# The relu of an ELU layer written to SBUF instead of its PSUM bank, in an attention + MLP kernel ordered by a planner

## The chip, the cores and the metric

One core of one Trainium2 chip runs the whole program. The metric is the device time of one execution in microseconds; a kernel is represented by the median of its runs. A profile of one execution shows every instruction of the five engines: PE (matmul), DVE (VectorE), ACT (ScalarE), POOL (GpSimd) and SP (DMA issue).

## The reference

The kernel computes block-sparse causal attention (4 batches, 8 heads, 768 tokens, head dimension 64; each query keeps 6 of 24 chunks of 32 keys) and feeds the result to a two-layer MLP with an ELU between the layers:

```
ub   = sum_d max(q*k_min, q*k_max)          # one bound per chunk
sel  = top 6 chunks by ub (causal)
attn = softmax(mask(q @ k.T / 8)) @ v
x    = attn, heads side by side              # 3072 x 512
h    = x @ w_in                              # 512 -> 2048
g    = where(h > 0, h, exp(min(h, 0)) - 1)   # ELU
out  = g @ w_out                             # 2048 -> 512
```

## The kernel before

The work is cut into units. A unit is a pair of heads of one batch; there are 16 of them, and each has two halves of 384 query rows. A unit's half goes through loading and transposing K and Q, the chunk bounds on PE (line 580), the top-6 selection on DVE (lines 597 to 620), copies on POOL that put the selection beside the bf16 operands (lines 548, 631), scores on PE (L672), exp on ACT (L699), the causal triangle on POOL (L718), the product with V on PE (L731), the division on DVE (L744, L747, tile `on`), and a transpose of the result (PE L756, ACT L759, tile `xT`). Counted over units and halves there are 32 operations `on`.

Four units make a batch. Its MLP runs in two halves of 384 rows. For each of 16 blocks of 128 hidden columns (`fc`) four matmuls make `h` in a PSUM bank (L781, tile `psH`; batch 3 takes two blocks at a time in a two-bank tile `psS`), ACT writes `e = exp(h)` to SBUF (L791), and the ELU is finished as `min(e - 1, relu(h))`. The result goes to `gT` in SBUF, from which the down projection (L838, tiles `psM`, `psMT`) reads 4 blocks per step, and ACT copies the sums out (L846). There are 96 such blocks in batches 0 to 2. Before the change they come in two forms, chosen by the table `BOTH`:

- in `BOTH` (48 blocks): ACT applies relu to the PSUM bank in place (L796), then one DVE operation reads `e` from SBUF and the bank (L799);
- otherwise (48 blocks): two DVE operations, each reading the bank (L820: `t = max(e - 1, h)`, L825: `gT = min(max(h, 0), t)`).

In both forms the bank is released by the last DVE operation (`free=bh + [e]`, `free=bh + [t]`). There are 3 banks of kind `H`, 3 buffers of `e`, 3 of `t` and 3 of `gT`. Batch 3 (`FAST`) uses a third form (L809, L814).

The order of all work is made by a planner (class `Plan`). Each step is added with an engine, an estimated duration, a rank `prio`, what it reads and writes, and which buffers it takes and frees. `order()` repeatedly starts the step that can start first, and among those that wait for one engine the one of lowest rank. Steps marked `port=True` and all POOL steps exclude each other in the plan; DVE steps without the mark run beside POOL. Instructions are then emitted in this order, and each engine's queue, the DMA queues of SP and POOL too, executes in order.

Of the kernel before, what the change touches and what calls it, by code (L numbers as in the profile page):

```python
# [10 lines left out]
AOT = mybir.AluOpType  # L11
AF = mybir.ActivationFunctionType
# [5 lines left out]
S = 768  # L18
# [10 lines left out]
HALF = S // 2  # L29
# [6 lines left out]
SPLIT = (0, 1, 2, 3)  # L36
GATES = {(2, 0): (0, 1, 2, 3), (2, 1): (4, 5, 6, 7)}

BOTH = {0: (0, 1, 4, 5, 8, 9, 12, 13), 1: (0, 1, 2, 3, 4, 5, 8, 9, 10, 11, 12, 13), 2: (1, 5, 9, 13), 3: ()}


def WHEN(q_in, left, out):
# [9 lines left out]
LATER = {4: 0}  # L52
RATES = (232.0, 232.0, -1.4, 0.75)
MERGE = (False, False, False, True)

DUMP = None

# [6 lines left out]
class Plan:  # L64
# [17 lines left out]
    def add(self, eng, dur, prio, emit, reads=(), writes=(), alloc=(), free=(), lat=None, tag="",  # L82
# [33 lines left out]
        self.ops.append(o)  # L116
        return o

    def order(self):
# [12 lines left out]
        waiting = {}  # L132
        for o in ops:
            waiting.setdefault(o.eng, [])
            engines[o.eng] = self.BEGIN
            if not o.left:
                waiting[o.eng].append(o)
        n_left = len(ops)
        port = {"POOL": 0.0, "DVE": 0.0}
        out = []  # L140
        while n_left:
            best = None
            for e, t in engines.items():
                cand = None
                for o in waiting[e]:
                    r = max(t, o.ready)
                    if o.port and o.eng in port:
                        r = max(r, port["DVE" if o.eng == "POOL" else "POOL"])
                    ok = True
                    for h in o.alloc:  # L150
                        fs = free_slots[h[0]]
                        if not fs:
                            ok = False
                            break
                        r = max(r, min(fs)[0])
                    if not ok:
                        continue
                    key = (r, o.prio, o.n) if r > t else (t, o.prio, o.n)
                    if cand is None or key < cand[0]:
                        cand = (key, o, r)  # L160
                if cand is not None and (best is None or cand[2] < best[2]):
                    best = cand
            assert best is not None, "no operation can start"
            _, o, r = best
            slots = []
            for h in o.alloc:
                fs = free_slots[h[0]]
# [24 lines left out]
            n_left -= 1  # L192
        return out
# [3 lines left out]
def kernel(  # L197
# [9 lines left out]
    nc = tc.nc  # L207
# [178 lines left out]
    def pair_prep(u):  # L386
# [52 lines left out]
        add("POOL", 0.13 + 0.00096 * S, pr + 1.0,  # L439
            lambda: nc.gpsimd.tensor_copy(out=tiles[vx][:, :, 0:D], in_=tiles[vd]),  # L440
            reads=[vd, "ones"], writes=[(vx, i) for i in range(2)], alloc=[vx], free=[vd])

    def first_prep(u, hf):
# [60 lines left out]
            return x.rearrange("q (j p) -> q p j", j=4)  # L504
        add("PE", TURN, pr, turn(bk, at_k), reads=[(hk, i0), "ident"], writes=[bk[0]], alloc=bk, free=fk)
        for hd in range(2):
            add("ACT", act(HALF), pr,
                lambda hd=hd: nc.scalar.activation(
                    out=tiles[kb][0:64, hd, a:b].rearrange("q (p j) -> q p j", j=4),
                    in_=tok(ps(bk, None, None)[64 * hd:64 * hd + 64, :]), func=AF.Copy),  # L510
                reads=[bk[0]], writes=[(kb, hf, hd), (bk[0], "turn")], alloc=[] if hf or hd else [kb])
# [26 lines left out]
        add("POOL", 0.13 + 0.00096 * HALF, pr + 1.0,  # L538
            lambda: nc.gpsimd.tensor_copy(
                out=tiles[vx].rearrange("p (h n) d -> p h n d", h=2)[:, :, 3 * hf:3 * hf + 3, 0:D],  # L540
                in_=tiles[sv][:, iv].rearrange("p (h n d) -> p h n d", h=2, d=D)),
# [3 lines left out]
    def cast(pr, w, what, **kw):  # L545
        def f():
            o, i = what()
            nc.gpsimd.tensor_copy(out=o, in_=i)  # L548
        add("POOL", 0.13 + 0.00096 * w, pr, f, **kw)

    def quad_sel(g, hf):

# [210 lines left out]
    def mlp(b, hf):  # L763
        tail = b == B - 1
        if True:
# [3 lines left out]
            for fc in range(0, NFC, step):  # L769
# [3 lines left out]
                def view(bh=bh):  # L773
                    return tiles[bh[0]][:, :, 0:HALF] if tail else ps(bh, [P, 1, HALF], F32)

                def up(view=view, fc=fc, c0=c0):
# [14 lines left out]
                    lambda e=e, view=view: nc.scalar.activation(  # L791
                        out=tiles[e][:, 0:step], in_=view(), func=AF.Exp),
                    reads=[bh[0]], writes=[(e, 0)], alloc=[e])
                if both:
                    add("ACT", act(step * HALF), pr,
                        lambda view=view: nc.scalar.activation(out=view(), in_=view(), func=AF.Relu),  # L796
                        reads=[bh[0]], writes=[bh[0]])
                    add("DVE", dve(step * HALF), pr,
                        lambda e=e, view=view, fc=fc, gt=gt: nc.vector.scalar_tensor_tensor(  # L799
                            out=tiles[gt][:, fc:fc + step, :], in0=tiles[e][:, 0:step], scalar=1.0, in1=view(),  # L800
                            op0=AOT.subtract, op1=AOT.min),
                        reads=[(e, 0), bh[0]], writes=[(gt, fc + i) for i in range(step)],
                        alloc=[gt] if fc == 0 else [], free=bh + [e])
                    continue
                t, = new("t")
                fast = FAST[b]
                if fast:
                    add("DVE", 0.32 + 0.00021 * step * HALF, pr,
                        lambda e=e, t=t: nc.vector.tensor_scalar(  # L809
                            out=tiles[t][:, 0:step], in0=tiles[e][:, 0:step], scalar1=1.0, scalar2=1.0,  # L810
                            op0=AOT.min, op1=AOT.subtract),
                        reads=[(e, 0)], writes=[t], alloc=[t], free=[e], port=True)
                    add("DVE", dve(step * HALF), pr,
                        lambda t=t, view=view, fc=fc, gt=gt: nc.vector.tensor_tensor(  # L814
                            out=tiles[gt][:, fc:fc + step, :], in0=tiles[t][:, 0:step], in1=view(), op=AOT.max),
                        reads=[t, bh[0]], writes=[(gt, fc + i) for i in range(step)],
                        alloc=[gt] if fc == 0 else [], free=bh + [t])
                    continue
                add("DVE", dve(step * HALF), pr,
                    lambda e=e, t=t, view=view: nc.vector.scalar_tensor_tensor(  # L820
                        out=tiles[t][:, 0:step], in0=tiles[e][:, 0:step], scalar=1.0, in1=view(),
                        op0=AOT.subtract, op1=AOT.max),
                    reads=[(e, 0), bh[0]], writes=[t], alloc=[t], free=[e])
                add("DVE", dve(step * HALF), pr,
                    lambda t=t, view=view, fc=fc, gt=gt: nc.vector.scalar_tensor_tensor(  # L825
                        out=tiles[gt][:, fc:fc + step, :], in0=view(), scalar=0.0, in1=tiles[t][:, 0:step],
                        op0=AOT.max, op1=AOT.min),
                    reads=[t, bh[0]], writes=[(gt, fc + i) for i in range(step)],
                    alloc=[gt] if fc == 0 else [], free=bh + [t])
            for tt in range(3):  # L830
                bm = bank("MT" if tail else "M")
                for part in range(4):
                    pr = mpos(b, hf) + 2 + 2 * (4 * tt + part) / 12

                    def down(bm=bm, tt=tt, part=part, gt=gt):
# [2 lines left out]
                            nc.tensor.matmul(pm, lhsT=tiles[gt][:, fc, 128 * tt:128 * tt + 128],  # L838
                                             rhs=w_out_sb[:, fc, :], start=(fc == 0), stop=(fc == NFC - 1))
                    add("PE", 4 * 0.2165, pr, down,  # L840
                        reads=[("w_out", part)] + [(gt, fc) for fc in range(4 * part, 4 * part + 4)],
                        writes=[(bm[0], part)], alloc=bm if part == 0 else [],
                        free=[gt] if tt == 2 and part == 3 else [])
                osb, = new("osb")
# [92 lines left out]
```

## Time and profile before

| | |
|---|---|
| median of 3 runs (lowest, highest) | 280.38 us (280.21, 285.49) |
| span of the profiled execution, first to last instruction | 278.4 us |
| outside the span (median less span) | 2.0 us |
| busy PE / DVE / ACT / POOL | 266.7 / 204.2 / 201.4 / 128.0 us |
| granted PE clock | full in all 40 slices |
| DMA | 29.82 MB, mean 107 GB/s |

The profiled execution has no separate time beside its span; the 2.0 us are taken as what lies around it. Busy times are unions of instruction intervals, so an engine whose instructions overlap by their pipelines can look fuller than it is. Idle time of an engine matters only where the engine that sets the end waits for it.

### The profile page before, as it was taken

The numbers are of one execution on the slowest core, as the hardware profiler recorded it, in microseconds if no ns is written. First come the engines' busy times: TensorE is split into PE (matmuls) and PEld (weight loads), VectorE is DVE, ScalarE is ACT, GpSimd is POOL, SyncE is SP. The second block draws the span as 40 slices with busy tenths as digits, with TensorE's granted clock in tenths as the row PEclk, the third lists the DMA queues.
The fourth block names the chain that finished last, engine by engine and source line by source line (L and its number), as shares of the span: only waits on it lengthen the run. The fifth ranks groups of instructions, "written<-read, shape, count | busy, mean of one in ns | idle before, by whom it ended". The sixth has DMA issues, their size and how long they took to land.

```text
span 278.4 us, 7242 instructions
## 1 busy us (share of the span) xinstructions
PE 266.7 (96%) x2732; PEld 164.0 (59%) x2732; DVE 204.2 (73%) x546; ACT 201.4 (72%) x381; POOL 128.0 (46%) x235
## 2 busy tenths in 40 slices
PE   7989899989999999999999999999999999999994
PEld 7968566644565556655665656565565556555541
DVE  6876965799999989999989588657856434767610
ACT  2879899946699697999899958685868564544311
POOL 5668863356797797966965625102320201000000
PEclk9999999999999999999999999999999999999999
DMA  7999999988998599999497101101101111101122
GB/s 187 232 211 188 197 203 207 146 131 163 189 171 156 73 143 201 165 163 170 87 164 114 38 2 38 40 0 40 39 4 38 40 39 40 38 0 40 38 75 75
DMA packets 111330, 29.82 MB, mean 107 GB/s; under 512 B 101056, under 2 KB 108224, under 8 KB 111296
## 3 DMA queue, kind: packets, MB, share of 16 engines
q1 hardware_dynamic: 106656, 24.78, 48.4%
q0 software_dynamic: 4224, 4.19, 9.2%
q8 instruction: 21, 0.34, 0.6%
q10 hardware_dynamic: 416, 0.39, 0.5%
q14 instruction: 13, 0.11, 0.1%
HBM read 27.26 MB, written 6.29 MB: 121 GB/s over the span
## 4 chain that ended last, share of the span: by engine, by line
PE 68%; ACT 15%; DVE 6%; DMA 4%; issue 3%; SPq 1%; POOL 0%; ACTq 0%; DVEq 0%
PE psM L838 20%; PE psH L781 15%; PE psS L781 7%; PE psMT L838 7%; PE psS L672 7%; ACT pt L699 7%; PE psO L731 5%; ACT e L791 3%; PE psS L580 3%; DMA gT<-in_v_dram 2%; DMA gT<-in_k_dram 2%; ACT psH L796 1%; ACT xT L759 1%; DVE gT L799 1%; PE psT L756 1%
## 5 line engine op out<-in xcount | busy, mean ns | idle before, releaser
L699 ACT ACTIVATE pt<-psS 128x768 bf16<-128x768 f32 (+1 forms) x120 | 91.5, 799 | 4.1 <-PE psS L672 2.6
L781 PE MATMUL psH<-xT,w_in_sb 128*128 128x384 bf16 x384 | 75.2, 325 | 1.6 <-ACT xT L759 0.9
L838 PE MATMUL psM<-w_out_sb,gT 128*128 128x512 bf16 x288 | 72.5, 379 | 0.4 <-DVE gT L825 0.2
L781 PEld LDWEIGHTS <-w_in_sb 128*128 128x128 bf16 x512 | 47.6, 97 | 34.8 <-issue 4.0
L791 ACT ACTIVATE e<-psH 128x384 f32<-128x384 f32 x96 | 48.3, 519 | 22.4 <-PE psH L781 21.9
L838 PEld LDWEIGHTS <-gT 128*128 128x128 bf16 x384 | 36.2, 98 | 35.0 <-DVE gT L825 0.6
L718 POOL TENSOR_SCALAR_AFFINE_SELECT pt<-pt 128x256 bf16<-128x256 bf16 (+1 forms) x56 | 29.0, 519 | 56.7 <-ACT pt L699 55.7
L672 PE MATMUL psS<-rhs,lhs 88*128 88x384 bf16 (+4 forms) x304 | 51.5, 283 | 1.6 <-ACT pt L699 0.9
L672 PEld LDWEIGHTS <-lhs 88*128 88x128 bf16 x304 | 27.8, 97 | 15.8 <-issue 1.5
L631 POOL COPY rhs<-selt 24x192 bf16<-24x192 bf16 (+2 forms) x56 | 25.5, 456 | 21.9 <-DVE selt L620 18.6
L799 DVE SCALAR_TENSOR_TENSOR gT<-e,psH 128x384 bf16<-128x384 f32 x48 | 25.6, 539 | 13.3 <-ACT psH L796 13.2
L731 PEld LDWEIGHTS <-pt 128*128 128x128 bf16 x672 | 27.8, 98 | 11.3 <-issue 3.8
L548 POOL CAST rhs<-qt 64x768 bf16<-64x768 f32 (+1 forms) x40 | 28.5, 711 | 12.3 <-ACT qt L526 6.1
L820 DVE SCALAR_TENSOR_TENSOR t<-e,psH 128x384 bf16<-128x384 f32 x48 | 25.9, 543 | 9.6 <-ACT e L791 9.2
L731 PE MATMUL psO<-vext,pt 128*128 128x65 bf16 x672 | 30.2, 194 | 1.7 <-DVE gT L799 1.1
L791 ACT ACTIVATE e<-psS 128x768 f32<-128x768 f32 x16 | 13.0, 810 | 19.0 <-PE psS L781 19.0
L825 DVE SCALAR_TENSOR_TENSOR gT<-psH,t 128x384 bf16<-128x384 f32 x48 | 25.9, 543 | 0.8
L796 ACT ACTIVATE psH<-psH 128x384 f32<-128x384 f32 x48 | 25.1, 528 | 0.0
L781 PE MATMUL psS<-xT,w_in_sb 128*128 128x384 bf16 x128 | 23.2, 326 | 0.0
L548 POOL CAST lhs<-kt 64x768 bf16<-64x768 f32 x24 | 19.6, 819 | 6.8 <-DVE kt L409 3.7
L838 PE MATMUL psMT<-w_out_sb,gT 128*128 128x512 bf16 x96 | 22.5, 379 | 0.0
L759 ACT ACTIVATE xT<-psT 128x384 bf16<-128x384 bf16 x32 | 16.5, 515 | 4.5 <-PE psT L756 4.4
(66 smaller groups left out, 293.4 us busy)
## 6 DMA issues: line engine op xcount, KB each, us to landing
out_dram<-osb SPq DMA_DIRECT2D x24, 256.0 KB, 2.0
vd<-in_v_dram SPq DMA_DIRECT2D x12, 384.0 KB, 5.2
stage<-in_k_dram SPq DMA_DIRECT2D x48, 96.0 KB, 3.4
stage<-in_q_dram SPq DMA_DIRECT2D x48, 96.0 KB, 3.6
w_in_sb<-in_moe_w_in_dram POOLq DMA_DIRECT2D x4, 512.0 KB, 11.5
w_out_sb<-in_moe_w_out_dram POOLq DMA_DIRECT2D x4, 512.0 KB, 8.8
gT<-in_v_dram SPq DMA_DIRECT2D x16, 96.0 KB, 4.3
gT<-in_k_dram SPq DMA_DIRECT2D x6, 192.0 KB, 5.5
```

What stands on the lines that cost most here:

```text
L548: nc.gpsimd.tensor_copy(out=o, in_=i)
L672: nc.tensor.matmul(p_s[:, hd, pc:pc + w], lhsT=tiles[pt_["kb"]][0:64 + NCH, hd, 128 * kb:128 * kb + 128], rhs=tiles[pt_["qb"]][0:64 + NCH, ...
L699: lambda bs=bs, pt=pt, wtot=wtot, lo=lo, at=at: nc.scalar.activation(out=tiles[pt][:, :, lo:lo + wtot], in_=tiles[bs[0]][:, :, at:at + wto ...
L718: nc.gpsimd.affine_select(out=a, in_=a, compare_op=AOT.is_ge, fill=0.0, base=0, pattern=pat, channel_multiplier=-1)
L731: nc.tensor.matmul(po[:, hd, qi, :], lhsT=tiles[pt][:, hd, off:off + 128], rhs=tiles[pt_["vx"]][:, 6 * hd + kb, :], start=(kb == 0), stop= ...
L781: nc.tensor.matmul(ph, lhsT=w_in_sb[:, kk, f0:f0 + 128], rhs=tiles[XT[4 * b + kk]][:, c0:c0 + HALF], start=(kk == 0), stop=(kk == NKK - 1))
L791: lambda e=e, view=view: nc.scalar.activation(out=tiles[e][:, 0:step], in_=view(), func=AF.Exp),
L796: lambda view=view: nc.scalar.activation(out=view(), in_=view(), func=AF.Relu),
L799: lambda e=e, view=view, fc=fc, gt=gt: nc.vector.scalar_tensor_tensor(out=tiles[gt][:, fc:fc + step, :], in0=tiles[e][:, 0:step], scalar=1 ...
L820: lambda e=e, t=t, view=view: nc.vector.scalar_tensor_tensor(out=tiles[t][:, 0:step], in0=tiles[e][:, 0:step], scalar=1.0, in1=view(), op0 ...
L825: lambda t=t, view=view, fc=fc, gt=gt: nc.vector.scalar_tensor_tensor(out=tiles[gt][:, fc:fc + step, :], in0=view(), scalar=0.0, in1=tiles ...
L838: nc.tensor.matmul(pm, lhsT=tiles[gt][:, fc, 128 * tt:128 * tt + 128], rhs=w_out_sb[:, fc, :], start=(fc == 0), stop=(fc == NFC - 1))
```

## The change

In batches 0 to 2 the relu of a block is now written to a `t` buffer in SBUF (bf16), by ACT for blocks in `BOTH` (line 839 of the changed kernel) and by DVE otherwise (line 843). The PSUM bank is freed by this relu. One DVE operation (line 847) then reads `e` and the relu, both from SBUF. `BOTH` is smaller: 32 blocks instead of 48. The planner gets 88 seeds (`SHIFTS`), each of which moves the rank of one window of steps or of all windows a little before the order is made; two duration estimates change (POOL copies from 0.00096 to 0.00084 us per element, and the ACT copy of K in batch 0 to 0.495 us), and the four parts of a down projection are made to depend on each other in turn. No other arithmetic changes, but the order of instructions does, on all engines and in the SP queue.

```diff
-BOTH = {0: (0, 1, 4, 5, 8, 9, 12, 13), 1: (0, 1, 2, 3, 4, 5, 8, 9, 10, 11, 12, 13), 2: (1, 5, 9, 13), 3: ()}
+BOTH = {0: (0, 4, 8, 12), 1: tuple(range(0, 16, 2)), 2: (1, 5, 9, 13), 3: ()}
+SHIFTS = (711345, 710489, 927914, ...
+    def shift(self, seeds):
+        ops = self.ops
+        n = len(ops)
+        for seed in seeds:
...
+            if draw() < 0.1:            # windows of 5 to 64 steps over the whole list
...
+                    for o in ops[j:j + w]:
+                        o.prio += m
...
+            else:                       # one window, of one engine in half of the draws
...
+                for o in ops[a:a + w]:
+                    if not one or o.eng == ops[a].eng:
+                        o.prio += m
     def order(self):
         ops = self.ops
+        self.shift(SHIFTS)
...
-                if both:
-                    add("ACT", act(step * HALF), pr,
-                        lambda view=view: nc.scalar.activation(out=view(), in_=view(), func=AF.Relu),
-                        reads=[bh[0]], writes=[bh[0]])
+                fast = FAST[b]
+                if both or not fast:
+                    r, = new("t")
+                    if both:
+                        add("ACT", act(step * HALF), pr,
+                            lambda view=view, r=r: nc.scalar.activation(out=tiles[r][:, 0:step], in_=view(), func=AF.Relu),
+                            reads=[bh[0]], writes=[r], alloc=[r], free=bh)
+                    else:
+                        add("DVE", dve(step * HALF), pr,
+                            lambda view=view, r=r: nc.vector.tensor_scalar(
+                                out=tiles[r][:, 0:step], in0=view(), scalar1=0.0, scalar2=None, op0=AOT.max),
+                            reads=[bh[0]], writes=[r], alloc=[r], free=bh)
                     add("DVE", dve(step * HALF), pr,
-                        lambda e=e, view=view, fc=fc, gt=gt: nc.vector.scalar_tensor_tensor(
-                            out=tiles[gt][:, fc:fc + step, :], in0=tiles[e][:, 0:step], scalar=1.0, in1=view(),
-                            op0=AOT.subtract, op1=AOT.min),
+                        lambda e=e, r=r, fc=fc, gt=gt: nc.vector.scalar_tensor_tensor(
+                            out=tiles[gt][:, fc:fc + step, :], in0=tiles[e][:, 0:step], scalar=1.0,
+                            in1=tiles[r][:, 0:step], op0=AOT.subtract, op1=AOT.min),
...
-                        alloc=[gt] if fc == 0 else [], free=bh + [e])
+                        alloc=[gt] if fc == 0 else [], free=[e, r])
...
-                    lambda e=e, t=t, view=view: nc.vector.scalar_tensor_tensor(
-                        out=tiles[t][:, 0:step], in0=tiles[e][:, 0:step], scalar=1.0, in1=view(),
-                        op0=AOT.subtract, op1=AOT.max),
-                    reads=[(e, 0), bh[0]], writes=[t], alloc=[t], free=[e])
...
```

More of the change, by code (lines that the diff above doesn't have):

```diff
@@ L54 @@
 MERGE = (False, False, False, True)
+SHIFTS = (711345, 710489, 927914, 266268, 840942, 852719, 674714, 873198, 676568, 189402, 749298, 506023, 526548,
[6 rows of a table added]
 DUMP = None
@@ L117, in add, with draw @@
         return o
+    def shift(self, seeds):
+        ops = self.ops
+        n = len(ops)
+        for seed in seeds:
+            x = [seed]
+            def draw():
+                x[0] = (6364136223846793005 * x[0] + 1442695040888963407) % 2 ** 64
+                return (x[0] >> 40) / 16777216.0
+            draw(), draw()
+            if draw() < 0.1:
+                amp = draw() * 0.8
+                j = 0
+                while j < n:
+                    w = 5 + int(draw() * 60)
+                    m = amp * (draw() - 0.5) * 2
+                    for o in ops[j:j + w]:
+                        o.prio += m
+                    j += w
+            else:
+                a = int(draw() * n)
+                v = draw()
+                w = 1 + int(v * v * v * 80)
+                amp = draw()
+                amp = 0.1 + 2.4 * amp * amp
+                m = amp * (draw() - 0.5) * 2
+                one = draw() < 0.5
+                for o in ops[a:a + w]:
+                    if not one or o.eng == ops[a].eng:
+                        o.prio += m
     def order(self):
         ops = self.ops
+        self.shift(SHIFTS)
         for o in ops:
@@ L438, in pair_prep @@
         fetch(0.5, 393.0, 205.0, pl + 1.2, vload, [vd], alloc=[vd], reads=late)
-        add("POOL", 0.13 + 0.00096 * S, pr + 1.0,
+        add("POOL", 0.13 + 0.00084 * S, pr + 1.0,
             lambda: nc.gpsimd.tensor_copy(out=tiles[vx][:, :, 0:D], in_=tiles[vd]),
@@ L506, in first_prep @@
         for hd in range(2):
-            add("ACT", act(HALF), pr,
+            add("ACT", 0.495, pr,
                 lambda hd=hd: nc.scalar.activation(
@@ L537, in first_prep @@
                  reads=[qt], writes=[(qb, hf, hd)], alloc=[] if hf or hd else [qb])
-        add("POOL", 0.13 + 0.00096 * HALF, pr + 1.0,
+        add("POOL", 0.13 + 0.00084 * HALF, pr + 1.0,
             lambda: nc.gpsimd.tensor_copy(
@@ L548, in f @@
             nc.gpsimd.tensor_copy(out=o, in_=i)
-        add("POOL", 0.13 + 0.00096 * w, pr, f, **kw)
+        add("POOL", 0.13 + 0.00084 * w, pr, f, **kw)
     def quad_sel(g, hf):
@@ new lines, in mlp @@
+                if both or not fast:
[9 more added lines that the diff above has]
+                            reads=[bh[0]], writes=[r], alloc=[r], free=bh)
+                    add("DVE", dve(step * HALF), pr,
+                        lambda e=e, r=r, fc=fc, gt=gt: nc.vector.scalar_tensor_tensor(
+                            out=tiles[gt][:, fc:fc + step, :], in0=tiles[e][:, 0:step], scalar=1.0,
+                            in1=tiles[r][:, 0:step], op0=AOT.subtract, op1=AOT.min),
+                        reads=[(e, 0), r], writes=[(gt, fc + i) for i in range(step)],
+                        alloc=[gt] if fc == 0 else [], free=[e, r])
@@ L804, in mlp @@
                     continue
                 t, = new("t")
[L806 to L818, printed above, removed]
@@ L819, in mlp @@
-                add("DVE", dve(step * HALF), pr,
-                    lambda e=e, t=t, view=view: nc.vector.scalar_tensor_tensor(
-                        out=tiles[t][:, 0:step], in0=tiles[e][:, 0:step], scalar=1.0, in1=view(),
-                        op0=AOT.subtract, op1=AOT.max),
-                    reads=[(e, 0), bh[0]], writes=[t], alloc=[t], free=[e])
[L824 to L827, printed above, removed]
+                add("DVE", 0.32 + 0.00021 * step * HALF, pr,
+                    lambda e=e, t=t: nc.vector.tensor_scalar(
+                        out=tiles[t][:, 0:step], in0=tiles[e][:, 0:step], scalar1=1.0, scalar2=1.0,
+                        op0=AOT.min, op1=AOT.subtract),
+                    reads=[(e, 0)], writes=[t], alloc=[t], free=[e], port=True)
@@ L828, in mlp @@
+                add("DVE", dve(step * HALF), pr,
+                    lambda t=t, view=view, fc=fc, gt=gt: nc.vector.tensor_tensor(
+                        out=tiles[gt][:, fc:fc + step, :], in0=tiles[t][:, 0:step], in1=view(), op=AOT.max),
                     reads=[t, bh[0]], writes=[(gt, fc + i) for i in range(step)],
@@ L840, in mlp @@
                     add("PE", 4 * 0.2165, pr, down,
-                        reads=[("w_out", part)] + [(gt, fc) for fc in range(4 * part, 4 * part + 4)],
+                        reads=[("w_out", part)] + [(gt, fc) for fc in range(4 * part, 4 * part + 4)]
+                        + ([(bm[0], part - 1)] if part else []),
                         writes=[(bm[0], part)], alloc=bm if part == 0 else [],
```

1 line of the change is left out of this document (removed), and 6 rows, old and new, of the table SHIFTS.

## The prediction

> **What bounds the kernel now.** I began with the page: the span, the busy shares and the 40 slices.
>
> ```profile
> span 278.4 us, 7242 instructions
> PE 266.7 (96%) x2732; PEld 164.0 (59%) x2732; DVE 204.2 (73%) x546; ACT 201.4 (72%) x381; POOL 128.0 (46%) x235
> PE   7989899989999999999999999999999999999994
> DVE  6876965799999989999989588657856434767610
> ACT  2879899946699697999899958685868564544311
> POOL 5668863356797797966965625102320201000000
> ```
>
> PE is full almost everywhere, so a shorter time must come from PE's few gaps, and any wait that makes PE idle is added to the end. DVE's row is the second thing to see: near 9 for the first half, loose after it. I then cut the span at PE's gaps and at two operations `on` (L747), the 8th and the 24th of the 32, which start where these rows begin.
>
> ```profile
> core 0: us, PE busy (x) PEld busy (x) DVE busy (x) ACT busy (x) POOL busy (x), PEclk, DMA share, GB/s
> 0.00:36.00 36.00, 32.40 (x568) 27.02 (x569) 27.34 (x109) 26.48 (x60) 25.63 (x61) 1.00 1.06 203
> 36.00:60.00 24.00, 21.95 (x234) 13.96 (x232) 16.71 (x35) 22.28 (x42) 11.39 (x20) 1.00 1.18 177
> 60.00:146.00 86.00, 83.77 (x931) 49.87 (x930) 81.54 (x228) 71.83 (x137) 66.17 (x113) 1.00 0.93 152
> 146.00:175.00 29.00, 29.00 (x272) 17.28 (x270) 22.80 (x62) 22.88 (x45) 13.81 (x23) 1.00 0.25 47
> 175.00:278.40 103.40, 99.54 (x736) 55.93 (x733) 55.84 (x116) 57.98 (x98) 10.97 (x20) 1.00 0.10 37
> ...
> 59.38 0.55 DVE L747 TENSOR_TENSOR on<-psO,rc 128x384 bf16<-128x384 f32 x1
> ...
> 174.65 0.56 DVE L747 TENSOR_TENSOR on<-psO,rc 128x384 bf16<-128x384 f32 x1
> ```
>
> Before 36 us loading and transposing set the pace. From 36 to 60 us ACT is full (22.28 of 24) and PE loses 2.05. From 60 to 146 us three engines share the load: PE idles 2.23 us, DVE is busy 81.54 of 86 (idle 4.46), POOL 66.17 (77%). From 146 us PE has no gap until its last instruction, so nothing lost before can be won back there. Only 2.05 + 2.23 = 4.3 us of idle PE time between 36 and 146 us, and 3.6 before, are there to be won; the tail after PE's last instruction stays.
>
> **The part that the change names: the bank.** The groups by line say what PE waited for ahead of an up projection, and what one operation of each kind lasts.
>
> ```profile
> L781 PE MATMUL psH<-xT,w_in_sb 128*128 128x384 bf16 x384 | 75.2, 325 | 1.6 <-ACT xT L759 0.9 <-DVE gT L799 0.2 <-DVE gT L825 0.2
> L799 DVE SCALAR_TENSOR_TENSOR gT<-e,psH 128x384 bf16<-128x384 f32 x48 | 25.6, 539 | 13.3 <-ACT psH L796 13.2
> L820 DVE SCALAR_TENSOR_TENSOR t<-e,psH 128x384 bf16<-128x384 f32 x48 | 25.9, 543 | 9.6 <-ACT e L791 9.2
> L825 DVE SCALAR_TENSOR_TENSOR gT<-psH,t 128x384 bf16<-128x384 f32 x48 | 25.9, 543 | 0.8
> L796 ACT ACTIVATE psH<-psH 128x384 f32<-128x384 f32 x48 | 25.1, 528 | 0.0
> ```
>
> PE idled 1.6 us in all before 384 matmuls, and the last DVE operation, which holds the bank, ended 0.4 us of that (L799 and L825). So releasing the bank early is worth 0.4 us directly. More is possible only through the new order, up to the 4.3 us above.
>
> **ACT and DVE.** `BOTH` goes from 48 to 32 blocks, so ACT loses 16 relus (0.53 us each by L796), and DVE gets 16 operations more: 160 instead of 144. In the 36 to 60 us stretch ACT carries 4 relus of batch 0 where it carried 8 (counted in the two orders between the 4th and 8th `xT`); 4 x 0.53 = 2.1 us of ACT. Part of PE's 2.05 us there follows ACT; I take 1.0 us of gain, bounds 0 and 2.
>
> For the middle I counted both instruction orders between the 8th and the 24th `on`. DVE has 34 + 22 + 22 = 78 MLP operations there before, and 32 relus + 55 `gT` = 87 after, and one more K/Q transpose. What they cost back to back, and what PE work moves, is read from starts.
>
> ```profile
> 36.23 0.56 DVE L825 SCALAR_TENSOR_TENSOR gT<-psH,t 128x384 bf16<-128x384 f32 x1
> 36.70 0.45 DVE L614 TENSOR_TENSOR selv<-ubt,thr 128x288 bf16<-128x288 f32 x1
> 37.07 0.55 DVE L820 SCALAR_TENSOR_TENSOR t<-e,psH 128x384 bf16<-128x384 f32 x1
> ...
> 140.06 0.33 PE psS L672 x2
> 140.39 0.65 PE psH L781 x4
> ...
> 141.37 0.86 PE psM L838 x4
> ...
> L427 DVE STREAM_TRANSPOSE qt<-stage 128x768 f32<-128x768 f32 x12 | 11.5, 955 | 0.2
> ```
>
> An operation that reads PSUM takes 0.47 us start to start. The new one reads two SBUF tiles, like L614: 0.37 us for 288 elements, plus 96 elements at 0.47/384 each, is 0.49 at most; so 0.47 serves for it and for the relu. Extra DVE work: 9 x 0.47 + 0.95 = 5.2 us, on 81.54 + 22.80 = 104.3, gives 109.5 us. PE work between the same marks falls: 16 matmuls `psM` (3.4 us) and 8 `psH` (1.3 us) fewer, 8 `psS` (1.3 us) more, in sum 3.4 us; half of it is done before the 8th `on` (8 `psM`, 1.7 us), half after the 24th (8 `psH` and 8 `psM` more, 8 `psS` less, 1.7 us). So the changed kernel breaks even if its 24th `on` starts 1.7 us before 174.65, at 172.9. Its 8th `on` comes at 59.4 + 1.7 - 1.0 = 60.1. Left between them are 112.8 us for 109.5 us of DVE work: 3.3 us of slack where DVE idled 4.46 us in 60 to 146 us alone. Some of that idling disappears when DVE is late anyway; with 2 us left the time would go down by 1.3 us, with all 4.46 up by 1.2.
>
> **The new wait: POOL.** In batches 0 to 2 no MLP operation of DVE read two SBUF tiles; now 96 do. The trace shows what such operations meet.
>
> ```profile
> 94.19 0.64 POOL L718 TENSOR_SCALAR_AFFINE_SELECT pt<-pt 128x512 bf16<-128x512 bf16 x1 [1.16 <-ACT pt L699]
> 94.43 0.70 DVE L614 TENSOR_TENSOR selv<-ubt,thr 128x288 bf16<-128x288 f32 x1
> ...
> 94.77 1.04 POOL L440 CAST vext<-vd 128x768 bf16<-128x768 f32 x1
> ...
> L614 DVE TENSOR_TENSOR selv<-ubt,thr 128x288 bf16<-128x288 f32 x6 | 3.1, 514 | 0.0
> ...
> L521 DVE TENSOR_TENSOR km<-kx,km x8: 121/223/508, 8.2 to 32.1; 128x12 f32<-128x12 f32 x8
> L747 DVE TENSOR_TENSOR on<-psO,rc x32: 511/550/559, 21.5 to 235.7; 128x384 bf16<-128x384 f32 x32
> ...
> L548 POOL CAST lhs<-kt 64x768 bf16<-64x768 f32 x19 | 15.6, 819 | 4.5 <-DVE kt L409 3.7
> L548 POOL CAST rhs<-qt 64x768 bf16<-64x768 f32 x18 | 14.8, 821 | 0.7
> L440 POOL CAST vext<-vd 128x768 bf16<-128x768 f32 x11 | 9.3, 845 | 1.4 <-PE psO L731 1.0
> L631 POOL COPY rhs<-selt 24x384 bf16<-24x384 bf16 x16 | 8.0, 500 | 3.0 <-DVE selt L620 2.3
> L718 POOL TENSOR_SCALAR_AFFINE_SELECT pt<-pt 128x512 bf16<-128x512 bf16 x12 | 7.6, 631 | 1.5 <-ACT pt L699 1.4
> L631 POOL COPY rhs<-selt 24x192 bf16<-24x192 bf16 x16 | 5.5, 346 | 3.8 <-DVE selt L620 3.2
> L718 POOL TENSOR_SCALAR_AFFINE_SELECT pt<-pt 128x256 bf16<-128x256 bf16 x12 | 4.9, 404 | 2.4 <-ACT pt L699 1.9
> ```
>
> L614 at 94.43, issued while a POOL operation ran until 94.83, took 0.70 us; the same form at 36.70 took 0.45. It ended 0.30 us after POOL's operation, as if it had waited for it, and POOL's next one, 1.04 us against a mean of 0.845, was stretched in turn. L521 handles 12 elements and still ranges from 121 to 508 ns. L747, the same kind of operation with one input from PSUM, stays between 511 and 559 ns in all its 32 places (minimum, median, maximum). So DVE operations with two SBUF inputs and POOL operations exclude each other here. L614 and L521 are marked `port=True`, so the planner keeps them apart from POOL as far as its estimates hold; the new L847 carries no mark.
>
> The Trainium skill has a rule for this: in SBUF — State Buffer, section Who interferes with whom, a DVE instruction with two SBUF inputs contends with a GpSimd instruction that reads SBUF, and whichever issues second is blocked until the other is done. The rows of L614 and L521 agree (0.70 against 0.45 us); no run shown yet has a SCALAR_TENSOR_TENSOR with two SBUF inputs. By the rule this forecast holds; were that operation exempt, the first rival below would.
>
> The price w of one such wait. Low end: L614 with 288 elements, 514 - 448 (the 0.45 row) = 0.07 us, although planned apart from POOL. High end: a DVE operation issued at random finds POOL busy in 77% of the cases, and waits for the rest of an operation. The seven POOL rows above (104 operations, mean 0.63 us) leave a rest of 0.35 us (half the mean square over the mean), so 0.27. I take 0.14, twice the low end since nothing keeps the new operations apart, and half the high end since POOL and DVE wait for each other in turn. Between the marks 55 such operations run: 55 x 0.14 = 7.7 us, ends 55 x 0.07 = 3.9 and 55 x 0.27 = 14.9. After 175 us POOL is busy 10.97 of 103.4 us, and the waits there cost nothing. Behind each wait stands DVE's whole queue: the relus that free the banks, the divisions that lead to `xT`, the transposes of the next units.
>
> **Sum.** 278.4 - 1.3 + 7.7 = 284.8 us of span; with the 2.0 us around it (median 280.38 less span) **286.8 us**. Ends: 278.4 - 1.3 + 3.9 + 2.0 = 283.0; 278.4 + 1.2 + 14.9 + 2.0 = 296.5, of which the top is unlikely as DVE's own idling (4.46) would be used first: 292.
>
> Other edits at no cost: the ACT relu waits for a `t` buffer, with exps behind it in ACT's queue, covered by ACT's idle time in the middle (86 - 71.83 = 14 us); if DVE is late this cover shrinks, which is inside the ends. The order of the SP queue changes, loads of V later and of K earlier by a few places in the first 20 us; bounds plus or minus 1 us, taken as zero. Estimates and the chain of parts change only the order.
>
> **Rivals.**
>
> 1. *No exclusion for the new operation* (or it falls in POOL's pauses). Then DVE's slack decides: 280.4 - 1.3 = 279.1 to 280.4 + 1.2 = 281.6; 280 us. For it: only TENSOR_TENSOR is seen waiting. Chance 0.22.
> 2. *Faster, by the ACT relief.* In 36 to 60 us ACT's relus go, and the new order fills PE's gaps until 146 us; all 4.3 us and some of the first 3.6 are won: 280.4 - 4.9 = 275.5. It decides if DVE is not late in the middle, so it too needs w near zero. For it: ACT 22.28 of 24. Against: DVE's slack of 3.3 us. Chance 0.10.
> 3. *POOL itself becomes the bound.* Between 60 and 146 us POOL works 66.17 us; 41 new operations run between the 8th and the 20th `on` in the changed order, 41 x 0.47 = 19.3. Together with 8 L614 at up to 0.45, that is 89.1 us of mutually exclusive work in 86. Then the casts and masks come late and scores wait for them; 3.1 us over, plus the 23% of POOL's time in which it waited for others, of which I take a third, 6.6: 280.4 + 9.7 = 290 us. Chance 0.12.
> 4. *The change does not do what it says*: the bank was hardly waited for (0.4 us). That is true in all cases above and has no time of its own.
>
> **How the numbers follow.** The forecast has 0.56, with its own range 282 to 292. Two per cent, 5.6 us, is about what a measurement of this kernel can tell from no change: 274.8 to 286.0 counts as the same. Slower: 0.36 of the forecast's 0.56 and rival 3, 0.48. Faster: 0.06, from rival 2. The same: 0.46. The range takes in rivals 1 and 2 at its lower end and rival 3 at its upper: 276 to 293.
>
> **What would show it.** Right: L847 lasts clearly longer on average between 60 and 146 us than after 175 us, with single ones near 0.8 to 0.9 us beside a POOL cast; DVE busy over 95% in the middle; PE idling there by 5 us or more, released by DVE; ACT below its 22.28 of 24 in 36 to 60 us; the 24th `on` after 178 us. Wrong: L847 with one duration whether POOL runs or not, and the 24th `on` at or before 173 us.

## The result and the profile after

The changed kernel takes 290.07 us (median of 4 runs, 289.57 to 290.79) against 280.94 us before (median of 4): slower by a factor of 1.0323, 95% interval 1.0279 to 1.0368. In some executions of most of these programs PE's granted clock drops to 0.5 to 0.6 for some 10 us between 14 and 30 us (0.58 from 20 to 30 us in the profile of experiment 2), and the kernel before then takes 283 to 286 instead of 280 to 283 us, so the experiments below are compared over the stretch that lies behind it, from the 8th to the 24th division `on`, beside their times. That stretch is read from one profiled execution of each program.

The page of the changed kernel, the same rows as before:

```profile
span 287.9 us, 7228 instructions
PE 269.9 (94%) x2732; PEld 164.4 (57%) x2732; DVE 225.0 (78%) x562; ACT 197.9 (69%) x365; POOL 143.4 (50%) x235
PE   8999899998888999799999899999999999999994
DVE  6796996799999979999989999784398526766620
```

DVE's busy time grew by 20.8 us, though 16 additional operations at about 0.47 us are only 7.5; POOL's grew by 15.4 us with the same 235 instructions. PE has new gaps between a fifth and a half of the span. The chain that ended last had 6% of DVE before and has 31% now (before, then after):

```profile
PE 68%; ACT 15%; DVE 6%; DMA 4%; issue 3%; SPq 1%; POOL 0%; ACTq 0%; DVEq 0%
...
PE 36%; DVE 31%; DMA 11%; POOL 7%; issue 6%; ACT 4%; SPq 4%; DVEq 0%; POOLq 0%; ACTq 0%
```

The windows cut at the same places as in the prediction, then one from the 8th to the 24th `on` (columns: busy time and count of PE, PE loads, DVE, ACT, POOL, then PE's granted clock), and the starts of these two; the last row is the same stretch before:

```profile
36.00:60.00 24.00, 23.11 (x242) 14.72 (x241) 19.27 (x38) 19.44 (x36) 10.72 (x18) 1.00 1.14 171
60.00:146.00 86.00, 78.23 (x802) 44.83 (x801) 83.42 (x207) 64.55 (x118) 65.64 (x101) 0.98 0.82 138
...
58.28:182.26 123.98, 113.81 (x1192) 66.21 (x1189) 120.52 (x300) 94.32 (x174) 93.24 (x138) 0.99 0.69 118
...
58.28 0.55 DVE L787 TENSOR_TENSOR on<-psO,rc 128x384 bf16<-128x384 f32 x1
...
182.26 0.54 DVE L787 TENSOR_TENSOR on<-psO,rc 128x384 bf16<-128x384 f32 x1
...
59.38:174.65 115.27, 112.91 (x1199) 67.20 (x1200) 104.61 (x291) 95.17 (x183) 80.31 (x136) 1.00 0.76 126
```

From 36 to 60 us PE's idle time fell from 2.05 to 0.89 us and ACT's load from 22.28 to 19.44: the relief of ACT came. From 60 to 146 us DVE is busy 97%, yet PE idles 7.77 us instead of 2.23. The stretch between the two marks, 115.27 us before, takes 123.98: 8.7 of the 9.5 us that the span grew by. The new operation, in the view of its line (duration minimum, median, maximum in ns) and in the groups between the marks, from 60 to 146 us, and from 175 to 278.4 us:

```profile
L847 DVE SCALAR_TENSOR_TENSOR gT<-e,t x96: 507/559/1226, 31.8 to 229.9; 128x384 bf16<-128x384 f32 x96
...
L847 DVE SCALAR_TENSOR_TENSOR gT<-e,t 128x384 bf16<-128x384 f32 x55 | 41.0, 762 | 0.3
...
L847 DVE SCALAR_TENSOR_TENSOR gT<-e,t 128x384 bf16<-128x384 f32 x37 | 28.1, 776 | 0.2
...
L847 DVE SCALAR_TENSOR_TENSOR gT<-e,t 128x384 bf16<-128x384 f32 x31 | 19.4, 637 | 4.7 <-ACT t L839 4.4
```

Its shortest is 507 ns and its longest 1226. The mean is 776 ns where POOL works 76% of the time (65.64 of 86 us) and 637 ns behind 175 us, where POOL works 20%. The timeline shows how it happens:

```profile
117.34 0.82 POOL L588 CAST lhs<-kt 64x768 bf16<-64x768 f32 x1
117.41 1.16 DVE L847 SCALAR_TENSOR_TENSOR gT<-e,t 128x384 bf16<-128x384 f32 x1
118.11 1.16 POOL L588 CAST rhs<-qt 64x768 bf16<-64x768 f32 x1
118.50 2.27 DVE L847 SCALAR_TENSOR_TENSOR gT<-e,t 128x384 bf16<-128x384 f32 x2
119.33 1.03 POOL L480 CAST vext<-vd 128x768 bf16<-128x768 f32 x1
121.66 0.99 DVE L843 TENSOR_SCALAR t<-psH 128x384 bf16<-128x384 f32 x2
122.24 1.90 PE L821 MATMUL psH<-xT,w_in_sb 128*128 128x384 bf16 x8 [2.00 <-DVE t L843]
```

DVE's operation starts 0.07 us after a POOL cast of 0.82 us and lasts 1.16 us. It ends 0.41 us after the cast. The next cast, begun at 118.11 while DVE still worked, lasts 1.16 us as well, and so on in turns. Behind three of these operations in DVE's queue stands the relu at 121.66 that frees a bank, and PE stands idle 2.00 us for it. PE's waits for that relu add up to 3.4 us, where PE had idled 0.4 us for a DVE operation that held a bank before:

```profile
PE psH L821 <- DVE t L843: 3.4, 5, 2.0
PEld L771 <- POOL pt L758: 3.4, 7, 0.8
PE psO L771 <- POOL pt L758: 1.8, 5, 0.5
PE psS L712 <- POOL rhs L671: 1.7, 4, 0.6
ACT e L831 <- DVE gT L847: 6.3, 13, 0.9
```

(Waiting engine and line, the one waited for, total us, times, longest.)

Between the marks PE idles 10.2 us (123.98 - 113.81) against 2.4 before; of these 10.2, waits that DVE ended make 5.8 us and waits that POOL ended 3.2. One other thing stands in this trace: behind the idle 2.00 us the granted clock is 0.57 from 123 to 127 us. The execution whose clock was full throughout took 289.57 us, the profiled one 289.99, so this is a small part of the 8.7 us at most.

### The profile page after: what moved, and what is told of

The parts are those of the page before. It is cut to its first block, busy times and chain, and to the rows that moved or that the text cites. A ratio compares the mean times of both kernels' runs of the same rounds, so it can differ in the third digit from the quotient of the medians.

```text
span 287.9 us, 7228 instructions
## 1 busy us (share of the span) xinstructions
PE 269.9 (94%) x2732; PEld 164.4 (57%) x2732; DVE 225.0 (78%) x562; ACT 197.9 (69%) x365; POOL 143.4 (50%) x235
## 4 chain that ended last, share of the span: by engine, by line
PE 36%; DVE 31%; DMA 11%; POOL 7%; issue 6%; ACT 4%; SPq 4%; DVEq 0%; POOLq 0%; ACTq 0%
DVE gT L847 9%; PE psM L872 8%; PE psS L821 7%; PE psMT L872 7%; PE psH L821 6%; DVE t L843 5%; PE psS L712 4%; DMA gT<-in_q_dram 3%; PE psO L771 3%; DVE thr L649 3%; POOL rhs L671 3%; DMA vd<-in_v_dram 3%; DVE qt L467 2%; DMA gT<-in_v_dram 2%; ACT pt L739 2%
## 5 line engine op out<-in xcount | busy, mean ns | idle before, releaser
L847 DVE SCALAR_TENSOR_TENSOR gT<-e,t 128x384 bf16<-128x384 f32 x96 | 65.5, 696 | 7.6 <-ACT t L839 6.8
L758 POOL TENSOR_SCALAR_AFFINE_SELECT pt<-pt 128x256 bf16<-128x256 bf16 (+1 forms) x56 | 33.9, 608 | 52.4 <-ACT pt L739 50.7
L712 PE MATMUL psS<-rhs,lhs 88*128 88x384 bf16 (+4 forms) x304 | 52.6, 284 | 2.2 <-POOL rhs L671 1.7
L843 DVE TENSOR_SCALAR t<-psH 128x384 bf16<-128x384 f32 x64 | 34.2, 542 | 13.5 <-ACT e L831 12.3
L671 POOL COPY rhs<-selt 24x192 bf16<-24x192 bf16 (+2 forms) x56 | 30.1, 538 | 20.3 <-DVE selt L660 17.9
L588 POOL CAST rhs<-qt 64x768 bf16<-64x768 f32 (+1 forms) x40 | 30.3, 758 | 12.6 <-ACT qt L566 6.3
L771 PEld LDWEIGHTS <-pt 128*128 128x128 bf16 x672 | 26.9, 98 | 10.1 <-POOL pt L758 3.4
L588 POOL CAST lhs<-kt 64x768 bf16<-64x768 f32 x24 | 20.9, 869 | 4.0 <-DVE kt L449 2.2
L855 DVE TENSOR_SCALAR t<-e 128x768 bf16<-128x768 f32 x16 | 8.9, 559 | 14.7 <-ACT e L831 14.7
L787 DVE TENSOR_TENSOR on<-psO,rc 128x384 bf16<-128x384 f32 x32 | 17.5, 546 | 0.3
## 6 DMA issues: line engine op xcount, KB each, us to landing
w_in_sb<-in_moe_w_in_dram POOLq DMA_DIRECT2D x4, 512.0 KB, 10.2
```

The lines of the kernel that those rows point to most:

```text
L671: eng.tensor_copy(out=dst.rearrange("c h (i two x) -> c h i two x", two=2, x=32)[:, :, :, odd, :], in_=tiles[st][r0:r0 + NCH, c0:c0 + n].r ...
L712: nc.tensor.matmul(p_s[:, hd, pc:pc + w], lhsT=tiles[pt_["kb"]][0:64 + NCH, hd, 128 * kb:128 * kb + 128], rhs=tiles[pt_["qb"]][0:64 + NCH, ...
L758: nc.gpsimd.affine_select(out=a, in_=a, compare_op=AOT.is_ge, fill=0.0, base=0, pattern=pat, channel_multiplier=-1)
L771: nc.tensor.matmul(po[:, hd, qi, :], lhsT=tiles[pt][:, hd, off:off + 128], rhs=tiles[pt_["vx"]][:, 6 * hd + kb, :], start=(kb == 0), stop= ...
L787: lambda rc=rc, on=on, bo=bo: nc.vector.tensor_tensor(out=tiles[on].rearrange("p q h d -> p h q d"), in0=ps(bo, None, None)[:, :, :, 0:D], ...
L843: lambda view=view, r=r: nc.vector.tensor_scalar(out=tiles[r][:, 0:step], in0=view(), scalar1=0.0, scalar2=None, op0=AOT.max),
```

## The experiments

The theory is that DVE operations with two SBUF inputs and POOL operations that read SBUF exclude each other, and that this turned a small gain into the loss. The rivals: the new order with DVE's added load, or writing the relu to SBUF as such.

**1. POOL no longer reads, in the changed kernel.** Edit (the same for the V copies and the selection rows):

```diff
-            nc.gpsimd.tensor_copy(out=o, in_=i)
+            nc.gpsimd.tensor_copy(out=o[:, 0:2], in_=i[:, 0:2])
+            nc.gpsimd.memset(o, 0.01)
```

> The changed kernel with the same order of instructions on all engines; only POOL's copies (K, Q, V casts and the selection rows) are replaced: each becomes a copy of two elements, which keeps its wait, and a memset of the whole output, so POOL still works about as long but hardly reads SBUF. The values of K, Q, V and the selection are left out by this. Theory (DVE operations with two SBUF inputs and POOL operations that read SBUF exclude each other): the mean of L847 falls from 696 to 550-600 ns, the 24th division starts near 175 us instead of 182.3, and the time is 279 to 284 us. Rival (DVE's additional work and the new order cost the time by themselves): L847 gets shorter or not, the time stays at 287 to 291 us. Second rival (any POOL operation excludes them, writing ones too): L847 stays near 690 ns and the time near 290.

Measured: 285.69 us (285.38 to 285.96), ratio to before 1.014 (1.0071 to 1.0208). The order of DVE, ACT, PE and SP was that of the changed kernel. The line, its group, and the window from the 8th to the 24th `on`:

```profile
L848 DVE SCALAR_TENSOR_TENSOR gT<-e,t x96: 505/548/1002, 34.4 to 225.7; 128x384 bf16<-128x384 f32 x96
L848 DVE SCALAR_TENSOR_TENSOR gT<-e,t 128x384 bf16<-128x384 f32 x96 | 53.1, 567 | 7.9 <-ACT t L840 7.1
...
60.56:177.24 116.68, 109.17 (x1170) 65.08 (x1182) 109.10 (x300) 93.34 (x172) 95.78 (x228) 1.00 0.72 126
```

POOL is as busy as in the changed kernel (95.78 against 93.24 us between the marks), but the operation is back at 567 ns in the mean, and the stretch takes 116.68 instead of 123.98 us. So it isn't POOL's being busy that stretches it but POOL's reading; the long ones that are left go with the masks (L718 before), which still read: all eight over 600 ns ran beside one. The time was above the expected 279 to 284 us; the control shows what the edit itself costs.

**2. Control: the same edit in the kernel before.**

> Control: the kernel before, order unchanged, with POOL's copies replaced as in the first experiment (a copy of two elements and a memset of the whole output; the values of K, Q, V and the selection are left out). Theory (exclusion with the new operation): here no MLP operation reads two SBUF tiles, so there is little to win: the stretch from the 8th to the 24th division stays at 114 to 116 us (115.2 before), where the same edit took the changed kernel's from 124.0 to 116.6. Rival (the edit helps by itself, as POOL is done sooner): that stretch falls by 4 to 7 us here too.

Measured: 287.24 us (285.63 to 289.49), ratio 1.0253 (1.0162 to 1.0345).

```profile
63.88:183.06 119.18, 112.16 (x1186) 67.45 (x1200) 104.80 (x290) 95.47 (x183) 89.11 (x228) 1.00 0.74 122
```

Expected was no change; the edit itself costs 3.9 us of the stretch (119.18 against 115.27), with 140 more POOL instructions in the program (375 against 235). So the rival that it helps by itself fell. With reading POOL the change adds 8.7 us to the stretch; with writing POOL it takes 2.5 us away (116.68 against 119.18). So the exclusion costs 7.3 us of the stretch if the edit is taken as free (123.98 - 116.68), and 11.2 us if it costs the changed kernel the same 3.9 us, which no run shows by itself. The whole times agree: the shortest executions are 289.57 and 280.21 us with reading POOL, and 285.38 and 285.63, no longer apart, with writing POOL.

**3. Two SBUF inputs, nothing else, in the kernel before.** All engines keep their order; 48 of the operations read a second SBUF tile. The edit, shortened to the calls that differ:

```diff
-  nc.scalar.activation(out=view(), in_=view(), func=AF.Relu)
+  nc.scalar.activation(out=tiles[r], in_=view(), func=AF.Relu)
...
-  in0=tiles[e][:, 0:step], scalar=1.0, in1=view(),
+  in0=tiles[e][:, 0:step], scalar=1.0, in1=tiles[r],
```

> The kernel before, with its order of instructions unchanged on all engines; only the 48 blocks whose relu is on ACT have it written to an SBUF buffer of its own, and their DVE operation reads two SBUF tiles instead of one and the bank. The bank is free for PE as soon as ACT is done. Theory (exclusion with POOL): these 48 operations go from 539 to 680-750 ns, 26 of them stand between 60 and 146 us, where DVE has 4.5 us idle, so 2 to 5 us more: 283 to 286 us. Rival (the early release of the bank is what counts): no longer operations, 280 us or 0.4 us less than before. Rival (order and DVE work alone cost the time): no change, 280 to 281 us.

**4. Its control:** the relu is still written to `r`, but DVE reads the bank.

> Control of the second experiment: the same program, instruction by instruction and with the relu of 48 blocks written to its own SBUF buffer, but their DVE operation reads the bank instead of that buffer (so the relu is left out of these blocks' result). One SBUF input, bank held until DVE is done. Theory (exclusion): these 48 operations are back at 535 to 555 ns (736 there), the stretch from the 8th to the 24th division at 114 to 116 us (119.1 there, 115.2 before), 280 to 282 us. Rival (the buffer r and the writing to SBUF by ACT cost the time): the stretch stays near 119 us, 283 to 285 us.

The two programs differ in one operand of 48 instructions. Experiment 3 and then 4, groups and marks:

```profile
L800 DVE SCALAR_TENSOR_TENSOR gT<-e,r 128x384 bf16<-128x384 f32 x48 | 35.1, 736 | 11.3 <-ACT r L797 11.2
...
64.20 0.55 DVE L747 TENSOR_TENSOR on<-psO,rc 128x384 bf16<-128x384 f32 x1
...
183.31 0.56 DVE L747 TENSOR_TENSOR on<-psO,rc 128x384 bf16<-128x384 f32 x1
```

```profile
L800 DVE SCALAR_TENSOR_TENSOR gT<-e,psH 128x384 bf16<-128x384 f32 x48 | 25.7, 540 | 13.2 <-ACT r L797 13.1
...
63.96 0.55 DVE L747 TENSOR_TENSOR on<-psO,rc 128x384 bf16<-128x384 f32 x1
...
179.10 0.56 DVE L747 TENSOR_TENSOR on<-psO,rc 128x384 bf16<-128x384 f32 x1
```

736 against 540 ns, and 119.11 against 115.14 us of stretch: 4.0 us for 48 operations, with order, instruction count and the writing by ACT equal. The control's 540 ns and 115.14 us are what the theory expected. Its stretch repeats the 115.27 us of the kernel before, so writing the relu to SBUF costs nothing there. The bank was held longer in the control, and it was the faster one. The medians, 288.03 us (284.33 to 289.6) and 284.56 us (280.18 to 285.46), are above the expected 283 to 286 and 280 to 282 us, but differ the same way, as the shortest executions do (284.33 and 280.18); the ratio of experiment 3 to before is 1.0144 (1.0022 to 1.0266).

**5. The change without the SBUF relu:** old operations, new table, estimates and seeds.

> The changed kernel with the MLP's operations of before (relu in place on ACT, or two DVE operations that read the bank), but the smaller table BOTH, the seeds and the new duration estimates; the planner makes its order anew. Theory (exclusion): no operation with two SBUF inputs in the MLP, so no stretched ones; DVE has 16 operations more than before, so 279 to 284 us. Rival (the shifted ranks or the load moved from ACT to DVE cost the time): 286 to 291 us.

Measured: 281.96 us (10 runs, 281.32 to 283.06), ratio 1.0018 (0.9983 to 1.0054). As the theory had it: the load moved to DVE and the shifted ranks cost nothing that can be seen. The stretch is 113.75 us, 1.5 less than before, though in an order of its own, since the planner made it anew.

**6 and 7. Without the seeds:** the changed kernel, and the old forms.

> The changed kernel without the seeds: the ranks aren't shifted, everything else as changed. Theory (exclusion): the new operations are stretched as before (mean 650-720 ns), 287 to 293 us; the seeds move single units but not this. Rival (the shifted ranks cost the time): 280 to 284 us.

> The MLP's operations of before, the smaller table BOTH and the new estimates, without the seeds. Theory: 280 to 284 us, the table and the estimates are worth little; with the seeds it was 281.96. Rival (the table BOTH, 16 operations more on DVE, costs time that the seeds won back): 284 to 288 us.

Measured: 295.71 us (293.73 to 296.31; ratio 1.0538, 1.0481 to 1.0595), with the operation at 687 ns in the mean, and 284.92 us (283.16 to 287.24; 1.017, 1.0083 to 1.0257). Both are 1 to 3 us above what I had expected, and the second lies in the range of its rival, that the table `BOTH` costs time which the seeds won back; that rival isn't excluded. The new form costs 8.1 us with the seeds (290.07 against 281.96) and 10.8 without. Over the stretch it is 10.2 us with them (123.98 against 113.75) and 6.4 without (122.95 against 116.58). By the stretch the seeds take 2.8 us off the old form and add 1.0 to the new one, while the times are 3.0 and 5.6 us shorter with them; what the seeds are worth so isn't settled.

**8. The new form in batch 2 alone**, where POOL has little to do.

> The changed kernel with the new form in batch 2 alone, whose MLP runs where POOL has little to do; batches 0 and 1 keep the MLP operations of before. Seeds, table and estimates as changed. Theory (exclusion only where POOL is busy): the 32 new operations are stretched less than 696 ns in the mean (560-620), and the time is 279 to 283 us, like the old forms in all batches. Rival (the new form costs wherever it stands): 284 to 287 us.

Measured: 284.39 us (283.14 to 287.75), ratio 1.0133 (1.0087 to 1.018). The 32 operations have a mean of 629 ns; both are above the expectation, and the time lies in the range of the rival, that the form costs wherever it stands. Fewer stretches than the 696 ns of all 96, but not none: the form gains nothing even there. How much of the 2.4 us over experiment 5 is the form and how much the order that the planner made for it was not separated. The trace speaks for the order: its stretch is 117.92 us against 113.75 in experiment 5, yet only 6 of the 32 operations stand in it, with a mean of 763 ns, which makes some 1.3 us by 6 x (763 - 548).

**9 and 10. The planner is told:** `port=True` on the new operation, with the seeds and without.

> The changed kernel with one word more: the DVE operation that reads e and the relu from SBUF is marked for the planner as excluding POOL; order made anew with the same seeds. Theory (exclusion, unplanned in the changed kernel): the planner moves POOL work and these operations apart, fewer of them are stretched (mean 580-650 instead of 696 ns), 283 to 288 us; it does not get to 280 because POOL and DVE together have too much exclusive work between 60 and 146 us. Rival (order and DVE work alone): 288 to 292 us.

> The changed kernel with the new DVE operation marked as excluding POOL, and without the seeds (they were drawn for a plan without the mark). If the seeds made the marked plan bad, 288 to 295 us, below the 295.71 of the unmarked kernel without seeds. If the exclusive work of POOL and DVE between 60 and 146 us is too much for any order (third rival of the prediction), 296 to 304 us as with the seeds.

Measured: 303.13 us (300.39 to 304.63; ratio 1.0748, 1.0655 to 1.0841) and 297.45 us (297.38 and 297.52; 1.0584, 1.0484 to 1.0683). The first expectation failed by 15 us; the second time lies in the range named for too much exclusive work, 296 to 304 us. With the mark the operations are still stretched (experiment 9):

```profile
L847 DVE SCALAR_TENSOR_TENSOR gT<-e,t 128x384 bf16<-128x384 f32 x96 | 63.0, 680 | 8.5 <-ACT t L839 7.6
```

680 ns against 696, and 656 against 687 without the seeds: the mark hardly separated them on the chip. Without the seeds, too, the mark gave no gain (297.45 against 295.71). Between the marks of experiment 9, 132.75 us, DVE idles 11.8 us where it idles 3.5 in the changed kernel, and the granted clock is 0.97, which can make up to 4 us (an estimate: 0.03 x 132.75). Why the marked order is worse, and not only no better, stays open; that the exclusive work is too much for any order fits, but no run shows it alone.

**11 and 12. Candidates:** the old operations with other seeds, drawn for their own plans, with the new and the old table.

> Candidate: the MLP's operations of before, the smaller table BOTH, other seeds, drawn for this plan. Theory (without two-SBUF operations the plan holds on the chip): a little better than with the seeds drawn for the new form (281.96), 278 to 281 us. Rival (small moves of ranks are lost on the chip): 281 to 284 us.

> Candidate: the MLP's operations and the table BOTH of before (48 relus on ACT), the new duration estimates, seeds drawn for this plan. Theory: 278 to 281 us. Rival: 281 to 284 us.

Measured: 282.31 us (278.03 to 283.14) beside 282.63 us (279.59 to 285.48) for the kernel before, and 283.59 us (280.49 to 288.24; ratio 1.0045, 0.9987 to 1.0103). Neither reached the expected 278 to 281 us. The lowest time of any kernel here, 278.03 us, is of the first candidate, but it is a single one of four executions; a version that beats both kernels isn't shown.

## Why the prediction was right, and what it mis-sized

The forecast was 286.8 us with 282 to 292 of its own, slower by POOL's exclusion of DVE; it was 290.07 us, for that reason. The named signs came: the new operation is longer between 60 and 146 us (776 ns) than behind 175 us (637), DVE is busy 97% there, PE idles 7.77 us, ACT carries 19.44 us from 36 to 60 us, and the 24th `on` starts at 182.26. One came in part: PE's idle time there was to be DVE's, and POOL ended about a third of it (2.5 us, DVE 4.1).

- **Bank.** Taken at 0.4 us of direct gain. No run shows it alone: in experiments 3 and 4 the stretch was 4.0 us longer with the bank free earlier, since the exclusion came with it. In the changed kernel PE waited more for banks (3.4 us), since the relu that frees them queues behind stretched operations.
- **ACT relief, 36 to 60 us.** Taken at 1.0 us; PE's idle time fell by 1.16 us. The 8th `on` came at 58.28 instead of the 60.1 that I had put down: 1.8 us better. I had charged the additional early down projections in full, and PE still had gaps for them: in the first 60 us it is busy 56.7 us instead of 54.3.
- **DVE's work between the marks.** 109.5 us predicted. Measured 120.52, less the stretch, 55 x (762 - 548 ns, the median of experiment 1) = 11.8: 108.7. Right within 0.8 us.
- **The price w of a wait: the term that was mis-sized.** I chose 0.14 us between 0.07 and 0.27; the 55 operations between the marks show 0.21, 11.8 us instead of 7.7. The low end came from operations that the planner keeps away from POOL, and weighing it equally was the error: the upper bound, a wait at a random moment of POOL's work, was the better guide for unplanned ones. Over all 96 the price is 0.15 (696 - 548), close to my 0.14 by luck: 26 of them stand after the 24th mark, where POOL has little to do.
- **DVE's own idle time.** 2 us assumed, 123.98 - 120.52 = 3.5 us measured.
- **After the 24th mark.** Predicted 1.7 us more PE work than before; the rest took 105.6 us (287.9 - 182.3) against 103.8, 1.9 more.
- **Sum of the differences to the predicted span of 284.8:** + 4.1 (w) - 1.8 (8th mark) + 1.5 (idle) - 0.8 (work) + 0.2 (rest) = 3.2, which but for rounding gives the 287.9. That some of the misses cancel is luck.
- **The rivals.** The first, no exclusion for this operation, fell with experiments 1 to 4; its size was about right: with a POOL that mostly writes the change takes 2.5 us off the stretch (experiments 1 and 2), and the old operations, in an order made for them with the new table and seeds, take 281.96 us where it had 279.1 to 281.6. The second, faster by the ACT relief, is true as to its place and was overrun. The third, POOL as a bound, is partly there: PE's matmuls waited 3.5 us for POOL's masks and rows (1.8 and 1.7 in the waits above; the 3.4 us of PEld run beside PE and aren't added), where before PE had no such wait in the list of its waits and PEld one of 0.2. POOL's operations are stretched too, so how much of this would be there without the exclusion isn't separated.
- **The cover named for ACT.** I had named the relu's wait for a `t` buffer as covered. What showed was an exp waiting for an `e` buffer that a stretched operation still held, 13 times, 6.3 us; ACT's idle time took it, as ACT stayed at 64.55 of 86 us in the middle.

The rule of the Trainium skill (SBUF — State Buffer, Who interferes with whom) held for SCALAR_TENSOR_TENSOR: 736 against 540 ns with one operand moved from PSUM to SBUF. It also says that a GpSimd instruction that only writes SBUF doesn't contend with such an operation, and experiment 1 agrees: 567 ns beside a POOL that mostly writes, 696 beside one that reads.

## What to carry to other kernels

Moving an operand from PSUM to SBUF wasn't free on DVE beside a busy POOL (540 to 736 ns): count the SBUF inputs of every operation, and price a second one at POOL's busy share times half a POOL operation, an estimate that gives 0.24 us here (0.77 x 0.63 / 2) where 0.20 and 0.21 were measured. Before freeing a resource early, look in the waits for how long anyone waited for it (0.4 us here). A planner that doesn't know of an exclusion can't plan for it; that it was told of it was no cure here (experiments 9 and 10).

## What the runs showed of the hardware that was not expected

Exclusion can go on in turns: a DVE operation that waits for a POOL cast makes the next cast wait, so that both engines slow down for several operations (1.16 us each for 0.55 and 0.82 us of work at 117 us). Single operations reached 1.9 us (1914 ns in experiment 3, 1936 in experiment 6), more than the rest of one POOL operation and their own 0.55 us together. The trace of experiment 3 shows what the first of them met:

```profile
87.32 0.82 POOL L548 CAST lhs<-kt 64x768 bf16<-64x768 f32 x1
87.41 1.91 DVE L800 SCALAR_TENSOR_TENSOR gT<-e,r 128x384 bf16<-128x384 f32 x1
88.09 0.82 POOL L548 CAST rhs<-qt 64x768 bf16<-64x768 f32 x1
```

It lay beside two casts in a row, neither of them stretched, and ended 0.41 us after the second (89.32 against 88.91), as the operation at 117.41 did after its one. So the turn doesn't always change after one POOL operation, and a wait can be longer than the rest of one. Why POOL had two turns here isn't known.
